# Later pairs of a chunk-attention and MoE kernel: the second product by one-level Strassen too, on weights' factors kept in DRAM

## The chip, the cores and the metric

One core of a Trainium2 chip. The time is the device time of one execution in microseconds (us); the metric is the median of the runs of each kernel. The engines are TensorE (PE), VectorE (DVE), ScalarE (ACT), GpSimd (POOL) and SyncE (SP), which issues all DMAs here.

## What is computed

Attention inside chunks of 64 tokens, then four experts, each weighted by a normalized probability:

```python
# q, k, v: (8, 8, 576, 64); N = 4608 tokens, D = 512, E = 4, F = 1024
scores = 1 / sqrt(64) * q_c @ k_c.T          # in each chunk of 64 tokens
attn = exp(scores - max); attn /= sum(attn) + 1e-9
x = (attn @ v_c) laid out as (4608, 512)
p = domain_probs / (domain_probs.sum(-1) + 1e-9)
for e in range(4):
    h = maximum(x @ w1[e], 0)
    out += p[:, e:e+1] * (h @ w2[e])
```

## The kernel before

The 4608 tokens are one sub-block of 512 and four **pairs** of two sub-blocks (pairs 0 to 3, 1024 tokens each). Half an expert (512 of its 1024 hidden columns) is one **pass**: eight passes for the first sub-block (`plain_pass`), then eight for each pair (`pair_pass`).

Every operand of a matmul is split into a high part, which ACT casts (`hi_part`, L210), and a low part, the difference, on POOL or DVE (`lo_part`, L213). A product of two operands is three matmuls for each block of 128 in the contraction: high x high, high x low, low x high (`TERMS`). A matmul streams 512 columns against a 128x128 block. `product` (L330) issues them all, so they have one line.

For a pair, x w1 is done by one-level Strassen in Winograd's form. The weights are cut into quadrants a11 to a22 with sums s1 to s4 (`Factors`, made by POOL in every pass), the tokens into b11 to b22 with differences t1 to t4 (`Tokens`). Seven products replace eight, each for two groups of 128 hidden columns (`Group(0)` is `g`, `Group(1)` is `h`): g.p1 to g.p7 and h.p1 to h.p7, six matmuls each, 84 in place of 96. The products accumulate in one bank (`self.a`) whose running sums ACT copies out on the way (`keep`, tiles s1, s2, s3; L386), and DVE adds them to other banks (`sum_parts`, L390). ACT and DVE then take ReLU and split the result (`relu_parts`, L339 and L340). The second product h w2 is plain: eight output tiles of 12 matmuls, whose result DVE multiplies by p and adds to `acc` (L462). So a pass of a pair has 84 + 96 = 180 matmuls. The weights of w1 and w2 are loaded and split anew in each pass.

The order is written out by hand. Each engine runs its instructions in the order in which they are issued. A pass is a list of PE steps, numbered from 0, and a table `at` that says behind which step the other work is issued; `issue` walks both. The last step of a pass (`held`) is issued as step 2 of the next one. `Beside` feeds in the attention of the next pair at a fixed rate, one piece at a time: scores, softmax, weights, transpose, values. All loads and stores go through SP's queue, in the order of issue. The PSUM banks come from one pool of six that rotates (`bank`).

## Time and profile before

| | |
|---|---|
| runs: median (lowest to highest) | 1590.95 us (1589.54 to 1591.47) |
| the profiled execution's own time | 1589.11 us |
| its span | 1587.3 us |
| matmuls of a pair's pass | 180 |
| DMA traffic | 123.13 MB, mean 78 GB/s |

The span runs from the first to the last instruction of the profiled execution; its own time has 1.8 us more around it. Rows of a timeline begin with the start in us and the duration; a row of a group has the operands (out <- in), the count, the busy time, the mean of one in ns, the idle time ahead of them and what ended it. The views that carry the argument are quoted in the prediction.

### The profile page before, as it was taken

How to read it: one execution, taken by the hardware profiler on the slowest of the kernel's cores; microseconds unless marked ns; L12 is line 12 of the kernel's file. 1: busy time of each engine (PE TensorE's matmuls, PEld its weight loads, DVE VectorE, ACT ScalarE, POOL GpSimd, SP SyncE). 2: the span in 40 equal slices, each digit the busy share in tenths (PEclk: the TensorE clock that was granted, in tenths of full speed). 3: DMA queues.
4: the chain of work that ended last, by engine and by line, in shares of the span. 5: the costliest groups of instructions: out<-in, count | busy, mean ns of one | idle time of the engine just before them, and what ended most of it. 6: DMA issues, size and time to landing. Idle time of an engine off the chain costs nothing.

```text
span 1587.3 us, 22072 instructions
## 1 busy us (share of the span) xinstructions
PE 1573.1 (99%) x9055; PEld 1285.5 (81%) x9056; DVE 733.1 (46%) x1038; ACT 583.2 (37%) x1037; POOL 737.1 (46%) x554
## 2 busy tenths in 40 slices
PE   7999999999999999999999999999999999999999
PEld 6877878888887888888888888888888888888887
DVE  5444554444444554444444644444444633333333
ACT  3343443333344443333333533333333433333332
POOL 2344574444444463444444744443344744444441
PEclk9999999999999999999999999999999999999999
DMA  5343341122221142221121232212211311111111
GB/s 195 120 140 120 102 151 57 63 74 74 74 74 46 34 147 74 86 75 51 56 73 54 81 139 74 73 50 72 73 54 53 100 48 51 45 51 53 53 40 53
DMA packets 43317, 123.13 MB, mean 78 GB/s; under 512 B 4304, under 2 KB 4688, under 8 KB 43216
## 3 DMA queue, kind: packets, MB, share of 16 engines
q1 hardware_dynamic: 43216, 121.73, 23.1%
q8 instruction: 71, 1.16, 0.3%
q14 instruction: 30, 0.25, 0.0%
...
## 4 chain that ended last, share of the span: by engine, by line
PE 92%; DVE 4%; ACT 2%; issue 1%; POOL 1%; DMA 1%; SPq 0%; POOLq 0%
PE ps L332 88%; PE psa L139 1%; PE psa L105 1%; PE psa L130 1%; DVE hl L340 1%; DVE e L171 1%; ACT hh L339 1%; DVE ps L390 1%; ACT s L386 0%; DMA xraw<-in_qk 0%; POOL w1l L213 0%; DVE z L169 0%; DVE z L164 0%; DMA wraw<-in_w 0%; ACT w1h L210 0%
## 5 line engine op out<-in xcount | busy, mean ns | idle before, releaser
L213 POOL TENSOR_TENSOR w2l<-wraw,w2h 128x512 fp32r<-128x512 f32 x160 | 211.9, 1341 | 629.1 <-ACT w2h L210 628.9
L332 PE MATMUL ps<-w2h,hh 128*128 128x512 f32 x1156 | 452.9, 392 | 0.0
L332 PE MATMUL ps<-w2h,hl 128*128 128x512 f32 x1156 | 449.3, 389 | 0.0
L332 PE MATMUL ps<-w2l,hh 128*128 128x512 f32 x1156 | 449.1, 389 | 0.0
L332 PE MATMUL ps<-xh,w1h 128*128 128x512 f32 (+1 forms) x1040 | 407.9, 393 | 0.6 <-ACT s L386 0.6
L332 PE MATMUL ps<-xh,w1l 128*128 128x512 f32 (+1 forms) x1040 | 401.9, 387 | 0.0
L332 PE MATMUL ps<-xl,w1h 128*128 128x512 f32 (+1 forms) x1040 | 400.1, 387 | 0.6 <-DVE xl L213 0.6
L462 DVE SCALAR_TENSOR_TENSOR acc<-ps,pr,acc 128x512 f32<-128x512 f32 (+1 forms) x253 | 187.4, 746 | 304.0 <-PE ps L332 303.8
L340 DVE SCALAR_TENSOR_TENSOR hl<-ps,hh 128x512 fp32r<-128x512 f32 (+1 forms) x292 | 199.2, 682 | 214.4 <-ACT hh L339 214.2
L213 POOL TENSOR_TENSOR w1l<-wraw,w1h 128x512 fp32r<-128x512 f32 x190 | 255.3, 1366 | 89.8 <-ACT w1h L210 88.0
L386 ACT COPY s<-ps 128x512 f32<-128x512 f32 x192 | 112.9, 588 | 443.1 <-PE ps L332 443.1
L339 ACT ACTIVATE hh<-ps 128x512 fp32r<-128x512 f32 (+1 forms) x292 | 173.2, 593 | 247.8 <-DVE ps L390 171.7
L332 PEld LDWEIGHTS ps<-w2h,hl 128*128 128x128 f32 x1156 | 217.0, 188 | 45.3
L332 PEld LDWEIGHTS ps<-w2h,hh 128*128 128x128 f32 x1156 | 217.0, 188 | 45.2
L332 PEld LDWEIGHTS ps<-w2l,hh 128*128 128x128 f32 x1156 | 217.1, 188 | 43.8
L390 DVE TENSOR_TENSOR ps<-ps,s 128x512 f32<-128x512 f32 x192 | 133.6, 697 | 256.0 <-ACT s L386 180.1
L332 PEld LDWEIGHTS ps<-xh,w1h 128*128 128x128 f32 x1040 | 195.7, 188 | 41.1 <-ACT s L386 1.1
L332 PEld LDWEIGHTS ps<-xh,w1l 128*128 128x128 f32 x1040 | 195.8, 188 | 40.0
L332 PEld LDWEIGHTS ps<-xl,w1h 128*128 128x128 f32 x1040 | 195.0, 189 | 38.7 <-DVE xl L213 1.0
L210 ACT CAST w1h<-wraw 128x512 fp32r<-128x512 f32 x192 | 112.0, 618 | 9.2 <-POOL wraw L242 8.7
L213 POOL TENSOR_TENSOR w1l<-ws,w1h 128x512 fp32r<-128x512 f32 x64 | 84.7, 1343 | 62.8 <-ACT w1h L210 62.7
L210 ACT CAST w2h<-wraw 128x512 fp32r<-128x512 f32 x160 | 95.1, 622 | 1.1 <-DMA wraw<-in_w 1.1
...
## 6 DMA issues: line engine op xcount, KB each, us to landing
wraw<-in_w SPq DMA_DIRECT2D x160, 512.0 KB, 4.0
qk_in<-in_qk SPq DMA_DIRECT2D x32, 512.0 KB, 5.2
out<-acc SPq DMA_DIRECT2D x35, 256.0 KB, 3.8
v_in<-in_v SPq DMA_DIRECT2D x32, 256.0 KB, 4.9
xraw<-in_qk SPq DMA_DIRECT2D x3, 512.0 KB, 10.2
qk_in<-in_v SPq DMA_DIRECT2D x2, 512.0 KB, 9.5
xraw<-in_qk SPq DMA_DIRECT2D x2, 256.0 KB, 2.7
...
```

The costliest lines, as they stand in the source:

```text
L105: nc.tensor.matmul(s["sc"][half, c, j], lhsT=s["x"][rows, g, 0, h], rhs=s["x"][rows, g, 1, h], start=True, stop=True,)
L130: nc.tensor.transpose(ps[:, j], s["e"][:, j].rearrange("p c k -> p (c k)"), ident)
L139: nc.tensor.matmul(av[half, c, j], lhsT=s["v"][rows, 2 * j + odd], rhs=s["pt"][rows, j, half], start=True, stop=True,)
L171: nc.vector.tensor_tensor(out=e, in0=e, in1=z.unsqueeze(2).broadcast_to([P, n, C]), op=ALU.mult)
L210: nc.scalar.copy(out=t[0], in_=src)
L213: eng.tensor_tensor(out=t[1], in0=src, in1=t[0].bitcast(F32), op=ALU.subtract)
L332: nc.tensor.matmul(out, lhsT=lhs(k, a), rhs=rhs(k, b), start=first and i == 0, stop=last and i == len(parts) - 1, skip_group_check=not (fi ...
L339: nc.scalar.activation(out=hi, in_=src, func=AF.Relu)
L340: nc.vector.scalar_tensor_tensor(out=lo, in0=src, scalar=0.0, in1=hi.bitcast(F32), op0=ALU.max, op1=ALU.subtract)
L386: nc.scalar.copy(out=t, in_=self.a)
L390: nc.vector.tensor_tensor(out=out, in0=p, in1=kept, op=ALU.add)
L462: nc.vector.scalar_tensor_tensor(out=o, in0=self.ps, scalar=p_e, in1=o, op0=ALU.mult, op1=ALU.add)
```

## The change

The first sub-block stays as it was but for the shape of its loads and the order in which pair 0's tokens are split. For pairs 1 to 3 the second product is done by Strassen as well, transposed: the output's columns stand on the partitions and the tokens are streamed. That has four parts.

- **Factors once.** In pair 0 (`first_pair_pass`) both w1's and w2's seven factors are made in each pass, split and stored in DRAM (`Factors.keep`): 14 slots of 512 KB for a pass, in the order in which they will be used (`ORDER`). The second product of pair 0 itself stays plain.
- **Streaming.** From pair 1 on nothing of the weights is made. `ring_load` fetches the slots through seven buffers `wf0` to `wf6`; when both halves of a slot have been used (`Units.done`), the load of the slot seven further on is issued.
- **p on h.** The outputs are summed over experts in `acc`, so p is multiplied into h: `Scaled.hidden` takes ReLU times p, where p lies as a row, broadcast over the partitions (`transpose_probs`, `probs_load`). DVE makes the differences t1, t3 and t2 (`sums`), POOL t4 (`last_sum`), ACT all high parts, POOL all low parts. `Outer` does the seven products (`a` for the first, `b` for the second 128 columns of a group) and DVE adds each running sum to `acc` (`Outer.add`). In a pair's first pass ACT copies it.
- **Outputs transposed last.** `outputs` transposes each tile of `acc` on PE, copies and stores it: in the first pass of the next pair, and for the last pair at the end (`last_outputs`).

The six banks now have names and fixed users. `a` and `g` use A0, B0 and C0, `b` and `h` A1, B1 and C1, but for p2's and p7's sums (B0 and B1). `qk_in` and `v_in` have one buffer each instead of two. A pass of pairs 1 to 3 has 168 matmuls, in the 34 steps of `later_pass` below; a step `x.p1(0)` is the first half of a product, three matmuls, and `x.p1(1)` the second.

```diff
-    ps = ctx.enter_context(tc.tile_pool(name="ps", bufs=6, space=bass.MemoryType.PSUM))
+    ps = ctx.enter_context(tc.tile_pool(name="ps", bufs=1, space=bass.MemoryType.PSUM))
-    def bank():
-        return ps.tile([P, SUB], F32, name="ps")
+    BANKS = ("A0", "A1", "B0", "B1", "C0", "C1")
+    turn = [0]
+    def bank(name=None):
+        if name is None:
+            name = BANKS[turn[0] % len(BANKS)]
+            turn[0] += 1
+        return ps.tile([P, SUB], F32, name=name)
...
+    def transpose_probs():
+        by_e = att.tile([P, n_exp, n_tiles], F32, name="e")
+        nc.vector.tensor_copy(out=by_e, in_=pr.rearrange("p t e -> p e t"))
+        by_e = by_e.rearrange("p e t -> p (e t)")
+        psa = ps_a.tile([P, 2, 2 * HG * C], F32, name="psa")
+        rows = att.tile([P, 2, P], F32, name="pt")
+        for i in range(2):
+            n = min(P, p_rows - i * P)
+            nc.tensor.transpose(psa[:n, i, :P], by_e[:, i * P : i * P + n], ident)
+            nc.scalar.copy(out=rows[:n, i], in_=psa[:n, i, :P])
+            nc.sync.dma_start(out=p_t[i * P : i * P + n, :], in_=rows[:n, i])
...
-                if step is a_scores and t + 1 < last:
-                    a_load(t + 1)
                 step(t)
+                if step is a_scores:
+                    a_load_v(t)
+                    if t + 1 < last:
+                        a_load(t + 1)
...
+    KEYS = {"a11": 0, "a12": 1, "a22": 2, "s1": 3, "s2": 4, "s3": 5, "s4": 6}
+    ORDER = [
+        (0, "a11", 0), (0, "a12", 0), (0, "s2", 0), (0, "s1", 0), (0, "a11", 1), (0, "s3", 0),
+        (0, "a12", 1), (0, "s2", 1), (0, "a22", 0), (0, "s4", 0), (0, "s1", 1), (0, "s3", 1),
+        (1, "a11", 0), (1, "a12", 0), (0, "a22", 1), (0, "s4", 1), (1, "a11", 1), (1, "s1", 0),
+        (1, "s1", 1), (1, "a12", 1), (1, "s2", 0), (1, "s2", 1), (1, "s4", 0), (1, "s3", 0),
+        (1, "s4", 1), (1, "s3", 1), (1, "a22", 0), (1, "a22", 1),
+    ]
+    PLACE = {unit: divmod(i, 2) for i, unit in enumerate(ORDER)}
+    N_RING = 7
+    RING = (0, 1, 4, 3, 5, 2, 6)
+    UNIT = [P, 2, 2, P]
+    slots = {
+        (n, i): dram.tile([P, 2, *UNIT[1:]], F32, name=f"w{n}_{i}")
+        for n in range(n_pass) for i in range(N_SLOT)
+    }
...
-        t = raw[i, piece] = wpool.tile([P, 2, HF], F32, name="wraw", bufs=3)
+        t = raw[i, f, k] = wpool.tile([P, 2, 2 * P], F32, name="wraw", bufs=N_RAW)
...
+        def hi(self, name):
+            k = KEYS[name]
+            tag = f"wf{k}"
+            pool = wpool
+            if self.i == 1:
+                tag, pool = f"hf{'hl'[k % 2]}6", hpool
+            t = self.made[name] = pool.tile([P, 2, *UNIT[1:]], F32R, name=tag)
+            parts = [t[:, :, part] for part in range(2)]
+            if self.i == 0:
+                w1t[k] = parts
+            hi_part(by_group(getattr(self, name)), parts)
+        def keep(self, n, name):
+            for g in range(2):
+                to = slot(n, self.i, name, g)
+                if name in self.made:
+                    nc.sync.dma_start(out=to, in_=self.made[name][:, g].bitcast(F32))
+                    continue
+                quad = w2_quad(int(name[1]) - 1, int(name[2]) - 1)
+                for part in range(2):
+                    nc.sync.dma_start(out=to[:, part], in_=quad[part][:, :, g * P : (g + 1) * P].bitcast(F32))
...
+    def ring_load(r):
+        if r < n_ring:
+            ring[r] = wpool.tile([P, 2, *UNIT[1:]], F32R, name=f"wf{RING[r % N_RING]}")
+            nc.sync.dma_start(out=ring[r].bitcast(F32), in_=slots[r // N_SLOT % n_pass, r % N_SLOT])
...
         def p1(self):
-            self.a = bank()
-            self.part(self.a, 0, 0, True)
+            self.a = bank(f"A{self.g}")
+            self.part(self.a, "a11", 0, True)
             self.s1 = self.keep("s1")
...
+    class Units:
+        def __init__(self, n):
+            self.first = (n - 2 * n_pass) * N_SLOT
+            self.left_over = {}
+        def done(self, i, name, g):
+            k, u = PLACE[i, name, g]
+            n = self.left_over[k] = self.left_over.get(k, 2) - 1
+            if n == 0:
+                ring_load(self.first + k + N_RING)
...
+        def hidden(self, src, s, f):
+            i, k = divmod(f, 2)
+            t = self.values[f"b{i + 1}{s + 1}", k] = wpool.tile([P, SUB], F32, name="wraw", bufs=N_RAW)
+            nc.vector.scalar_tensor_tensor(
+                out=t, in0=src, scalar=0.0, in1=self.pb[:, s], op0=ALU.max, op1=ALU.mult
+            )
+        def sums(self, k):
+            self.less("t1", "b12", "b11", k, nc.vector)
+            self.less("t3", "b22", "b12", k, nc.vector)
+            self.less("t2", "b22", "t1", k, nc.vector)
+        def last_sum(self, k):
+            self.less("t4", "b21", "t2", k, nc.gpsimd)
+        def hi(self, name, k):
+            nc.scalar.copy(out=self.part(name, 0)[:, k], in_=self.value(name, k))
+        def lo(self, name, k, eng=None):
+            (eng or nc.gpsimd).tensor_tensor(
+                out=self.part(name, 1)[:, k], in0=self.value(name, k),
+                in1=self.part(name, 0)[:, k].bitcast(F32), op=ALU.subtract,
+            )
...
+        def sum_parts(self, out, p, kept, s, f):
+            nc.vector.tensor_tensor(out=out, in0=p, in1=kept, op=ALU.add)
+            self.hidden(out, s, f)
...
+        def part(self, out, name, right, first, last, ks=(0, 1)):
+            left = self.left(1, name, self.g)
+            product(
+                out, [part for part in PARTS if part[0] in ks],
+                lambda k, a: left[a][:, k], lambda k, b: self.h.part(right, b)[:, k],
+                first=first and 0 in ks, last=last and 1 in ks,
+            )
+            if 1 in ks:
+                self.left.done(1, name, self.g)
+        def add(self, src, i, s):
+            key = self.n // n_pass, 2 * i + self.g + NK * s
+            if key not in acc:
+                acc[key] = opool.tile([P, SUB], F32, name=f"acc{key[1]}")
+                nc.scalar.copy(out=acc[key], in_=src)
+            else:
+                nc.vector.tensor_tensor(out=acc[key], in0=src, in1=acc[key], op=ALU.add)
...
+        def p6(self, *ks):
+            self.part(self.a, "s2", "t2", False, False, ks)
+            if 1 in ks:
+                self.add(self.a, 0, 1)
+        def p4(self):
+            self.part(self.a, "a22", "t4", False, True)
+            self.add(self.a, 1, 0)
...
+    def outputs(pair, i, out_ps, stage, eng=None):
+        s, j = divmod(i, NT)
+        o = out_ps.rearrange("p (m d) -> p m d", d=P)
+        for m in range(NK):
+            nc.tensor.transpose(o[:, m], acc[1 + pair, m + NK * s][:, j * P : (j + 1) * P], ident)
+        if eng is None:
+            nc.scalar.copy(out=stage, in_=out_ps)
+        else:
+            nc.vector.tensor_copy(out=stage, in_=out_ps)
+        t = (1 + pair * PAIR) * NT + i
+        nc.sync.dma_start(out=out[t * P : (t + 1) * P, :], in_=stage)
...
+        for i, name in enumerate(KEYS):
+            add(at, 1 + i, lambda name=name: made.keep(n, name))
+        w2 = Factors(1)
+        add(at, 0, w2.sum1, w2.sum2)
+        add(at, 3, lambda: w2_split(0, 0), lambda: w2_split(0, 1))
+        add(at, 4, lambda: w2_split(1, 0), w2.sum3)
+        add(at, 5, lambda: w2_split(1, 1), w2.sum4)
+        for i, name in enumerate(("s1", "s2", "s3", "s4")):
+            add(at, 6 + i, lambda name=name: w2.hi(name), lambda name=name: w2.lo(name))
+            add(at, 8 + i, lambda name=name: w2.keep(n, name))
+        for i, name in enumerate(("a11", "a12", "a22")):
+            add(at, 13 + i, lambda name=name: w2.keep(n, name))
+            add(at, 3, lambda: w_load(0, n + 1, 0, 0), lambda: w_load(0, n + 1, 0, 1))
+            add(at, 7, lambda: w_load(0, n + 1, 1, 0))
+            add(at, 10, lambda: w_load(0, n + 1, 1, 1))
...
+    def probs_load(pair, e):
+        t = pb[pair, e] = wpool.tile([P, PAIR, SUB], F32, name="ws")
+        r = e * n_tiles + (1 + pair * PAIR) * NT
+        nc.sync.dma_start(
+            out=t.rearrange("p s t -> p (s t)"),
+            in_=p_t[r : r + PAIR * NT, :].rearrange("t p -> (t p)").partition_broadcast(P),
+        )
+    ASIDE = (1, 4, 7, 24, 26, 29, 32)
...
+        steps = [
+            g.p1, g.p2, held, g.p6, g.p5, h.p1, g.p7, h.p2, h.p6, g.p4, g.p3, h.p5, h.p7,
+            lambda: a.p1(0), lambda: a.p2(0), h.p4, h.p3,
+            lambda: a.p1(1), lambda: b.p1(0, 1), lambda: a.p5(0), lambda: b.p5(0),
+            lambda: a.p2(1), lambda: b.p2(0, 1), lambda: a.p6(0), lambda: b.p6(0),
+            lambda: a.p5(1), lambda: b.p5(1), lambda: a.p6(1), lambda: b.p6(1),
+            a.p3, a.p7, b.p3, b.p7, a.p4,
+        ]
...
+        hi(3, "b11", 0)
+        lo(3, "b11", 0)
+        hi(8, "b22", 0)
+        hi(8, "b11", 1)
...
+        add(at, 11, lambda: sc.sums(0))
+        hi(11, "t1", 0)
+        hi(11, "t2", 0)
+        lo(11, "t1", 0)
+        lo(11, "t2", 0)
+        hi(13, "b22", 1)
+        lo(13, "b22", 1)
+        hi(15, "b21", 1)
+        lo(15, "b21", 1)
+        add(at, 16, lambda: sc.sums(1))
...
+        for k in range(2):
+            hi(18, "t3", k)
+            lo(18, "t3", k)
+        for k in range(2):
+            add(at, (12, 22)[k], lambda k=k: sc.last_sum(k))
+            hi((14, 22)[k], "t4", k)
+            lo((14, 22)[k], "t4", k)
...
+        if first_pass and pair > 1:
+            def output(i):
+                stage = att.tile([P, SUB], F32, name=("e", "pt")[i % 2])
+                psa = ps_a.tile([P, 2, 2 * HG * C], F32, name="psa")
+                outputs(pair - 1, i, psa[:, 0], stage)
+            for i in range(PAIR * NT):
+                add(at, (4, 7, 10, 13, 16, 19, 22, 24)[i], lambda i=i: output(i))
...
+        for i, step in enumerate(steps):
+            if step is not None:
+                step()
+            for f in at.get(i, ()):
+                f()
+            if i in ASIDE and not first_pass:
+                beside.go()
+        return b.p4, late
+    def last_outputs():
+        pair = n_pairs - 1
+        ws = wpool.tile([P, 2, SUB], F32, name="ws")
+        stages = [hpool.tile([P, SUB], F32, name=name, bufs=1 + (name == "s2")) for name in ("s1", "s2", "s2", "s3")]
+        stages += [ws[:, 0], ws[:, 1]]
+        stages += [att.tile([P, SUB], F32, name=name) for name in ("e", "pt")]
+        for j, i in enumerate((4, 5, 6, 7, 0, 1, 2, 3)):
+            eng = nc.vector if i < NT and i % 2 else None
+            outputs(pair, i, bank(("B0", "B1", "C0", "C1")[j % NT]), stages[j], eng)
```

In the rows below a matmul names out <- moving operand, stationary operand; numbers behind a name tell tiles apart, and what stands in brackets are the semaphores it waits for: those of DVE, ACT (Activation), POOL, PE or of a DMA (DMAHW).

PE where one pass ends and the next begins, before: the end of a tile (the moving operand is w2), then g.p1 on its own bank.

```order
L332 MATMUL ps_13080<-w2h3_12867,hh13_12953 128x512
L332 MATMUL ps_13080<-w2l3_12868,hh13_12953 128x512
L332 MATMUL ps_13080<-w2h3_12867,hl13_12954 128x512
L332 MATMUL ps_13094<-xh0_10981,w1h0_12916 128x512 [waits DVE_49]
L332 MATMUL ps_13094<-xl0_10982,w1h0_12916 128x512
```

The same place now, between two passes of the last pair: the end of a.p4 and the start of g.p1.

```order
L427 MATMUL A0_13676<-hfh3_13686,wf6_13747 128x512 [waits Activation_49]
L427 MATMUL A0_13676<-hfl3_13688,wf6_13747 128x512 [waits Pool_49]
L427 MATMUL A0_13676<-hfh3_13686,wf6_13747 128x512
L427 MATMUL A0_13828<-xh0_11418,wf0_13706 128x512 [waits DMAHW3_49,DVE_49]
L427 MATMUL A0_13828<-xl0_11419,wf0_13706 128x512
```

The two tiles A0_13676 and A0_13828 are the same bank; DVE's add of the former stands between them.

ACT around h.p7 (the copy to `s3`), before: the ReLU of g.p3's result and casts of the next pass's weights are ahead of it.

```order
L339 ACTIVATE hh02_13215<-ps_13094 128x512 [waits PE_49]
L210 CAST w1h0_13228<-wraw_13103 128x512 [waits DMAHW0_49]
L339 ACTIVATE hh10_13238<-ps_13143 128x512 [waits DVE_49]
L210 CAST w1h1_13244<-wraw_13167 128x512 [waits DMAHW1_49]
L386 COPY s3_13254<-ps_13154 128x512 [waits PE_49,Activation_49]
```

Now, in a pass of the last pair (hfh4 and hfh5 are the high parts of t1 and t2 of h, hfh1 of b21):

```order
L596 CAST hfh1_13936<-wraw_13934 128x512 [waits DVE_49]
L596 CAST hfh4_13961<-wraw_13847 128x512 [waits DVE_49]
L596 CAST hfh5_13963<-wraw_13900 128x512 [waits DVE_49]
L488 COPY s3_13978<-A1_13879 128x512 [waits PE_49,Activation_49]
L596 CAST hfh2_13922<-wraw_13981 128x512 [waits DVE_49]
```

All three casts ahead of the copy now wait for DVE.

ACT in a pass of pair 0, steps 6 to 9, now (before, no such rows stood there): hfl6 and hfh6 hold the factors of w2 in turn, s1 and s3 in hfl6, s2 and s4 in hfh6; hfh1 is the ReLU of g.p4.

```order
L271 CAST hfl6_3692<-ws_3585 128x2x256 [waits DMAHW6_49,Pool_49]
L161 COPY pt_3700<-psa_3695 128x512 [waits PE_49]
L434 ACTIVATE hfh3_3710<-B1_3686 128x512 [waits DVE_49]
L271 CAST hfh6_3716<-ws_3585 128x2x256 [waits DMAHW2_49,Pool_49]
L488 COPY s2_3727<-A1_3666 128x512 [waits PE_49]
L434 ACTIVATE hfh0_3621<-B0_3702 128x512 [waits DVE_49]
L271 CAST hfl6_3733<-wraw_3526 128x2x256 [waits DMAHW7_49,DMAHW6_49,Pool_49]
L434 ACTIVATE hfh1_3742<-A0_3586 128x512 [waits PE_49]
```

The second cast into hfl6 waits for the DMAs that store the first one's result, and the ReLU stands behind it.

## The prediction

> **What bounds the kernel now.** The page comes first: the engines' shares of the span, and the chain that ended last.

> ```profile
> span 1587.3 us, 22072 instructions
> PE 1573.1 (99%) x9055; PEld 1285.5 (81%) x9056; DVE 733.1 (46%) x1038; ACT 583.2 (37%) x1037; POOL 737.1 (46%) x554
> PE 92%; DVE 4%; ACT 2%; issue 1%; POOL 1%; DMA 1%; SPq 0%; POOLq 0%
> ```

> PE is busy throughout and is 92% of the chain; each other engine is idle more than half the time. So the time is the number of matmuls times their pace, and a change moves it by taking matmuls away or by making PE wait. The timeline of PE in a late pass gives the pace: 95 matmuls lie between these two starts (the rows between are evenly spaced).

> ```profile
> 1319.78 0.39 PE L332 MATMUL ps<-w2l,hh 128*128 128x512 f32 x1
> ...
> 1341.31 0.39 PE L332 MATMUL ps<-xh,w1h 128*128 128x512 f32 x1
> ```

> (1341.31 - 1319.78) / 95 = 0.2266 us per matmul; 0.39 is a duration, and durations overlap. A pass of 180 matmuls takes 40.8 us, and one of 168 would take 38.1.

> **Removed: matmuls.** In pairs 1 to 3 (24 passes) the second product takes 14 x 6 = 84 matmuls where it took 96. 24 x 12 x 0.2266 = **-65.3 us**. Splitting the weights in these passes goes too, but POOL and ACT did it beside PE, so that is worth nothing by itself.

> **Added: transposes.** 24 output tiles of four transposes each, all PE work. The chain in order of time shows four such in the attention, and the hand-over from DVE to PE just ahead:

> ```profile
> 590.39 1.51 DVE e L171
> 592.04 0.63 PE psa L130 x4
> 592.67 6.85 PE ps L332 x30
> ```

> 24 x 0.63, and 0.3 for the probabilities: **+15.4 us**. DVE ends at 591.90 and PE starts at 592.04: 0.14 us from DVE to PE.

> **Added: a wait at each pass boundary.** Step 33 (`a.p4`) ends in bank A0 and the next pass's step 0 (`g.p1`) begins in A0, so PE waits for DVE's add of that bank into `acc`. Before, the banks rotated and the last one was long free. The timeline gives the hand-overs:

> ```profile
> 1338.85 0.70 DVE L390 TENSOR_TENSOR ps<-ps,s 128x512 f32<-128x512 f32 x1 [2.02 <-PE ps L332]
> 1339.58 0.60 ACT L339 ACTIVATE hh<-ps 128x512 fp32r<-128x512 f32 x1 [1.56 <-DVE ps L390]
> 1341.09 0.39 PE L332 MATMUL ps<-w2h,hl 128*128 128x512 f32 x1
> 1341.51 0.75 DVE L462 SCALAR_TENSOR_TENSOR acc<-ps,pr,acc 128x512 f32<-128x512 f32 x1 [1.97 <-PE ps L332]
> ```

> DVE starts 0.42 after the start of the last matmul; add 0.70, hand back 0.14: 1.26 instead of 0.23, a wait of 1.03. 23 boundaries: **+23.7 us** (bounds 21 and 28, the latter where DVE is late).

> **Added: `h.p4` (step 15) waits for ACT.** It accumulates in A1, which ACT must first copy to `s3` after `h.p7` (step 12). In ACT's order two casts of step 11 now stand ahead of that copy, and the second waits for the last of five DVE operations behind `g.p3` (step 10): the add, ReLU times p, and the sums t1, t3, t2.

> ```profile
> L386 ACT COPY s<-ps 128x512 f32<-128x512 f32 x192 | 112.9, 588 | 443.1 <-PE ps L332 443.1
> L210 ACT CAST w1h<-wraw 128x512 fp32r<-128x512 f32 x192 | 112.0, 618 | 9.2 <-POOL wraw L242 8.7
> ...
> L340 DVE SCALAR_TENSOR_TENSOR hl<-ps,hh x292: 416/692/694, 23.2 to 1565.9; 128x512 fp32r<-128x512 f32 x142, 128x256 fp32r<-128x256 f32 x4
> ...
> L171 DVE TENSOR_TENSOR e<-e,z x34: 691/693/1506, 11.9 to 1195.5; 128x512 f32<-128x512 f32 x34
> L213 DVE TENSOR_TENSOR xl<-xraw,xh x13: 1225/1712/2371, 198.3 to 1244.6; 128x1024 fp32r<-128x1024 f32 x13
> L213 POOL TENSOR_TENSOR w1l<-wraw,w1h x190: 1267/1296/2282, 12.0 to 1528.4; 128x512 fp32r<-128x512 f32 x190
> ```

> The last four are of the views of single lines, with min/median/max in ns. From the start of `g.p3`'s last matmul: 0.42 + 0.70 + 0.69 + 3 x 0.69, then the cast 0.62, the copy 0.59 and about 0.15 of hand-overs make 5.24. Without the wait `h.p4` starts 19 matmuls later, at 4.31. So PE waits at least 0.93 us. The sums read two SBUF operands while POOL runs, and there the DVE rows spread: 1225 to 2371 ns, 1.15 more at most, median 0.5 more. Three sums at the worst row give 0.93 + 3 x 1.15 = 4.4, but POOL stands still between two of them (it waits for the cast of t1), so two, 3.2, is my upper bound. I take 1.6, one sum between median and worst: 24 x 1.6 = **+38.4 us** (22 to 77).

> [...]

> **Added: `a.p2(1)` (step 21) waits for POOL.** Per pass POOL now makes 14 low parts and two differences. Back to back they take 1.27 each:

> ```profile
> 1344.05 2.54 POOL L213 TENSOR_TENSOR w2l<-wraw,w2h 128x512 fp32r<-128x512 f32 x2 [18.35 <-ACT w2h L210]
> ```

> That is 20.3 us of 38.1, so POOL is no bound, but its order is. From t1's cast (65 x 0.2266 to the start of `g.p3`'s last matmul, then 0.42 + 0.70 + 0.69 + 0.69 and a cast of 0.62: about 18.0 us into the pass) stand six operations up to b21's second low part: 18.0 + 6 x 1.27 = 25.6, and two or three sums push it back by 0.5 to 1.1 each, to 26.6 to 28.9. PE reaches that low part after 112 matmuls, 25.4, and the 1.6 of step 15: 27.0. I take 0.4, near the low end: **+9.6 us** (0 to 46).

> **Moved: attention between the steps.** DVE's share of a tile, from the timeline:

> ```profile
> 236.69 0.68 DVE L115 TENSOR_REDUCE m<-psa 128x8 f32<-128x512 f32 x1
> 237.41 0.69 DVE L116 TENSOR_TENSOR e<-psa,m 128x512 f32<-128x512 f32 x1
> ...
> 244.21 0.68 DVE L164 TENSOR_REDUCE z<-e 128x8 f32<-128x512 f32 x1
> ...
> 245.75 1.49 DVE L171 TENSOR_TENSOR e<-e,z 128x512 f32<-128x512 f32 x1
> ```

> Softmax takes 1.4, the weights 3.0 (244.21 to 247.24). Six passes of pairs 1 and 2 carry them after steps 1, 4, 7, 24, 26, 29, 32. Behind step 7 stand b21 and the chain of t2, behind 26 the add that frees A0, behind 32 the add at the boundary. By the rate of the issue a pair meets these places some six times, at about 1 us each beyond what the waits above already cover: I take **+10 us** (0 to 20) for both pairs, and **+4** (0 to 10) for the two passes in which the next pair's tokens are split on the same engines.

> **Added in the first pair: ACT waits for a DMA.** Its passes keep 180 matmuls, but make and store both weights' factors. w2's s1 and s3 share one buffer, so ACT's cast of s3 (step 8) waits until s1 lies in DRAM, and behind that cast stands the ReLU of `g.p4`, which `begin(0)` (step 13) needs. POOL's first low part stands 1344.05 - 1335.87 = 8.2 us into the pass of before:

> ```profile
> 1335.87 0.39 PE L332 MATMUL ps<-xh,w1h 128*128 128x512 f32 x1
> ...
> out<-acc SPq DMA_DIRECT2D x35, 256.0 KB, 3.8
> wraw<-in_w SPq DMA_DIRECT2D x160, 512.0 KB, 4.0
> ```

> Seven POOL operations (8.9), a store (3.8, as `out`), a cast and a ReLU (1.2) end at 22.1. PE wants that ReLU after 87 matmuls, at 19.7. The wait is 2.4; eight passes, **+19.2 us** (0 if POOL starts early, 32 if the store takes 1.6 more, behind w1's stores).

> **The end** loses its half-width tile and gains copies and 256 KB stores behind the last transposes: **+2 us** (0 to 5).

> **Hidden: the stream.** Each later pass loads 14 x 512 KB, 191 GB/s in 38.1 us. A load is issued when its buffer's last user has run, six slots of twelve matmuls ahead (16 us; 11 for the slot that is freed latest), and takes 4.0. On SP they stand in one order with the attention's loads; the longest holder is the next pair's first `qk_in` load (step 30 of a last pass), which waits some 8 us for POOL's low part of t1 in the next pass, less than the lead. Transfers overlap, in the view of busy time by stretch:

> ```profile
> 22.00:23.00 1.00, 1.00 (x10) 1.00 (x10) 0.00 (x0) 1.00 (x3) 0.00 (x0) 1.00 1.04 397
> ```

> The last number is 397 GB/s, the one before it the DMA engines' share. Cost 0; without overlap, 14 x 4.0 = 56 us a pass (a rival below).

> **Sum** against this execution's own 1589.1 us: -65.3 + 15.4 + 23.7 + 38.4 + 9.6 + 10 + 4 + 19.2 + 2 = +57.0, so 1646.1. The median of the runs shown, 1590.95, is 1.8 higher: **1648 us**. All terms low give 1584, all high 1759.

> **Rivals.**
> *The waits stay at their floor (faster).* If the sums never meet POOL, the wait at step 15 is 0.93, the boundary 0.9, all others 0: -65.3 + 15.4 + 20.7 + 22.3 = -6.9, **1584**. It decides by PE's wait per later pass: with the first pair hidden too, the change wins below 49.9 / 24 = 2.1 us. For it: POOL works only 20.3 us of a pass. Against it: boundary and step 15 alone come to 1.96 at their cheapest.
> *POOL and DVE hold each other up.* Steps 15 and 21 near their upper ends, 3.0 and 1.2: 24 x 2.2 more than taken, **1701**. For it: the 2371 ns row.
> *The clock falls in the waits.* At the start of before, after gaps of PE, the granted clock (last number but two) fell; first the timeline of PE, then the stretches after the gap:

> ```profile
> 26.67 0.63 PE L512 MATMUL ps<-ident,e 128*128 128x128 f32 x4 [2.15 <-DVE e L171]
> ```

> ```profile
> 27.00:28.00 1.00, 1.00 (x8) 1.00 (x7) 0.96 (x2) 0.00 (x0) 0.00 (x0) 0.66 0.92 311
> 28.00:29.00 1.00, 1.00 (x7) 1.00 (x6) 0.18 (x1) 0.79 (x2) 0.00 (x0) 0.50 0.35 139
> 29.00:30.00 1.00, 0.73 (x4) 0.43 (x3) 0.34 (x1) 1.00 (x4) 0.57 (x1) 0.50 0.00 0
> 30.00:31.00 1.00, 0.84 (x20) 0.84 (x22) 0.97 (x3) 0.91 (x3) 1.00 (x2) 0.63 0.00 0
> ```

> A gap of 2.15 us with little beside it cost at most 0.34 + 0.50 + 0.50 + 0.37 = 1.7 us of clock. Once in each of 32 passes: +54, **1702**. Against it: the waits here are mostly 1 to 1.6 us, with 13 us of matmuls between them. [...]
> *The stream binds.* 56 us a pass instead of 41.1: 24 x 14.9 more, **2006**. The 397 GB/s speak against it.

> **Chances.** Forecast (1605 to 1685) 0.66; floor 0.12, of which 0.05 within 0.2%; POOL and DVE 0.12; clock 0.07; stream 0.03. A difference of 0.2%, 3.2 us, is about what a measurement of this kernel can tell from none. Faster 0.08, same 0.05, slower 0.87. The range leaves out the floor, the stream and a few of the highest: **1592 to 1708**.

> **What would show it.** In the profile after: among the waits PE <- DVE `acc` about 23 times 1.0; PE <- ACT `s3` 24 times 1 to 2; PE <- POOL low part under 1; in the first pair PE <- ACT ReLU, eight times 2.4; the clock at 9 throughout; DMA near 200 GB/s with no PE wait on it. The forecast is wrong if PE's idle time in a later pass without attention is below 2 us or above 5.

## The result, and the profile after

| | before | after |
|---|---|---|
| median of the runs (lowest to highest) | 1590.24 us (1586.45 to 1591.47) | 1796.05 us (1793.55 to 1798.35) |
| the profiled execution: span | 1587.3 us | 1792.9 us |

The ratio is 1.1298, with a 95% interval of 1.1272 to 1.1325: the change makes the kernel 13% slower. The prediction had the sign, but 1648 us, and its range ended at 1708.

The page of after, the same lines as of before (spans, busy time and share of each engine, the granted clock of PE in 40 slices, the shares of the chain):

```profile
span 1792.9 us, 23418 instructions
...
PE 1607.1 (90%) x8853; PEld 1272.2 (71%) x8854; DVE 964.6 (54%) x1301; ACT 572.3 (32%) x997; POOL 857.3 (48%) x645
...
PEclk9999989999999999998999899998999899999999
...
PE 15%; DVE 3%; issue 0%; ACT 0%; DVEq 0%
```

Of the page before, the row of the clock:

```profile
PEclk9999999999999999999999999999999999999999
```

There are 202 PE instructions less, yet PE is busy 34 us longer and idle 186 us instead of 14. The idle time shows waits, and a busy time that grows while the work shrinks shows a lower clock: the 8s in its row (over the whole span 0.96 of full speed, 1.00 before). The chain is followed back over only 18% of the span here, so it says little, and the waits have to be read instead. Who PE waited for (total, times, longest):

```profile
PE A L427 <- ACT s L488: 54.0, 24, 3.5
PE A L427 <- DVE acc L645: 27.9, 29, 2.0
PE A L427 <- DVE hfl L435: 22.5, 8, 7.5
PE psa L159 <- DVE e L200: 11.3, 6, 2.6
PE psa L740 <- ACT e L742: 7.3, 2, 3.6
PE A L427 <- DVE acc L720: 6.9, 7, 2.9
...
PE B L427 <- POOL hfl L599: 6.1, 4, 2.6
...
PE psa L98 <- DVE e L92: 4.7, 1, 4.7
```

Three of them are the prediction's own: step 15 (ACT `s`), the boundary (DVE `acc`, L645) and the first pair's ReLU (`hfl`). The others are the attention (`psa` L159), the transposed outputs (L740), boundaries up to and in the first pair (L720) and the transposes of the probabilities (L98).

By stage: busy time of each engine (number of instructions behind it), the granted clock, the DMA engines' share and GB/s, of the first sub-block, pair 0, and pairs 1 to 3, each from the first matmul of its first pass:

```profile
0.00:229.90 229.90, 214.07 (x1644) 171.95 (x1646) 114.36 (x162) 84.18 (x151) 98.61 (x76) 0.98 0.39 123
229.90:622.20 392.30, 360.90 (x1995) 287.61 (x1994) 163.62 (x234) 146.15 (x259) 228.40 (x178) 0.97 0.67 225
622.20:1021.50 399.30, 347.25 (x1884) 270.64 (x1883) 241.71 (x319) 116.47 (x199) 182.95 (x132) 0.95 0.51 168
1021.50:1427.80 406.30, 354.87 (x1921) 277.20 (x1922) 240.78 (x319) 121.16 (x207) 181.84 (x133) 0.94 0.52 170
1427.80:1792.90 365.10, 330.00 (x1414) 264.79 (x1414) 204.07 (x267) 104.38 (x182) 165.52 (x129) 0.97 0.52 169
```

The first number behind the stretch is its length, the next PE's busy time; the difference is idle. The same stages before:

```profile
0.00:223.40 223.40, 214.79 (x1657) 172.90 (x1659) 113.83 (x161) 83.58 (x149) 98.52 (x76) 0.98 0.37 126
223.40:565.00 341.60, 340.52 (x1969) 277.56 (x1968) 163.81 (x232) 131.76 (x234) 169.00 (x126) 1.00 0.23 74
565.00:909.60 344.60, 344.14 (x1985) 280.90 (x1984) 164.68 (x233) 130.17 (x231) 165.21 (x123) 1.00 0.23 74
909.60:1254.30 344.70, 344.26 (x1986) 280.97 (x1985) 164.59 (x233) 130.18 (x231) 165.14 (x123) 1.00 0.23 74
1254.30:1587.30 333.00, 329.40 (x1465) 273.16 (x1463) 126.23 (x179) 107.54 (x193) 139.20 (x110) 1.00 0.16 55
```

Against the prediction's terms, put into their stages:

| stage | predicted | measured | PE idle after |
|---|---|---|---|
| first sub-block | +0.3 | +6.5 | 15.8 |
| pair 0 | +19.2 | +50.7 | 31.4 |
| pair 1 | +9.1 | +54.7 | 52.1 |
| pair 2 | +14.2 | +61.6 | 51.4 |
| pair 3 and the end | +14.2 | +32.1 | 35.1 |
| sum | +57.0 | +205.6 | 185.8 |

**One pass without attention**, a quiet pass below (the fourth of pair 3), tells most of it. It took 43.90 us, where 41.1 was predicted (38.1 and the waits 1.03, 1.6 and 0.4) and 40.8 stood before. The same columns as above for this pass, and below it for the second pass of the pair, which has no stretch at half clock:

```profile
1564.94:1608.84 43.90, 40.58 (x168) 32.44 (x168) 25.57 (x34) 11.71 (x20) 20.30 (x16) 0.96 0.57 181
1477.87:1521.00 43.13, 39.13 (x168) 31.21 (x168) 25.80 (x33) 12.10 (x21) 21.24 (x16) 1.00 0.55 185
```

First its waits; the timeline around step 15 (start, duration, and in brackets the idle time ahead and what ended it):

```profile
1578.72 3.80 POOL L599 TENSOR_TENSOR hfl<-wraw,hfh 128x512 fp32r<-128x512 f32 x3 [5.52 <-ACT hfh L596]
...
1581.86 3.76 DVE L583 TENSOR_TENSOR wraw<-wraw 128x512 f32<-128x512 f32 x3
1583.10 0.62 ACT L596 CAST hfh<-wraw 128x512 fp32r<-128x512 f32 x1 [2.79 <-DVE wraw L583]
1583.80 1.27 POOL L599 TENSOR_TENSOR hfl<-wraw,hfh 128x512 fp32r<-128x512 f32 x1 [1.28 <-ACT hfh L596]
1585.65 0.62 ACT L596 CAST hfh<-wraw 128x512 fp32r<-128x512 f32 x1 [1.93 <-DVE wraw L583]
1586.18 0.58 ACT L488 COPY s<-A 128x512 f32<-128x512 f32 x1
1586.81 0.50 PE L427 MATMUL A<-xh,wf 128*128 128x512 f32 x1 [2.52 <-ACT s L488]
```

The queue is the one foreseen: two casts, then the copy to `s3`, then PE. The size is not. Three sums of 0.69 took 3.76: alone, their rows show 1.21, 0.69 and 1.72. POOL's three low parts run until 1582.52, and the first sum, begun at 1581.86, ends 0.55 after them: it was held for 0.52. The third begins at 1583.89, just behind POOL's low part of t1 (1583.80 to 1585.07), and again ends 0.55 after POOL, at 1585.62: held for 1.03. So the wait is 0.93 + 0.52 + 1.03 = 2.5; PE shows 2.52, and its first matmul takes 0.1 longer to be followed.

Then the clock. In this profile the 34 stretches at half clock (0.50) are one, two or three times 3.413 us long, but for the last of them, and all start on one grid of that step. Two passes of the last pair, cut along that grid (last number but two: the granted clock):

```profile
1583.85:1587.26 3.41, 0.90 (x4) 0.43 (x4) 2.20 (x2) 1.10 (x2) 2.13 (x2) 1.00 0.54 159
1587.26:1590.67 3.41, 3.41 (x10) 2.63 (x9) 1.61 (x3) 1.70 (x3) 3.32 (x4) 0.50 0.00 0
1495.10:1498.51 3.41, 2.11 (x10) 1.41 (x8) 3.27 (x3) 0.62 (x1) 1.60 (x2) 1.00 0.61 195
1498.51:1501.92 3.41, 2.21 (x10) 1.83 (x11) 1.85 (x4) 1.82 (x4) 2.61 (x3) 1.00 0.05 20
1501.92:1505.34 3.42, 3.42 (x17) 2.84 (x16) 2.65 (x5) 1.37 (x3) 3.42 (x3) 1.00 0.44 141
```

The same wait of 2.5 us stands in both. In the first two rows it falls into one cell of the grid, PE is busy for 0.90 of it, and the next cell runs at half clock (10 matmuls, where the fifth row, busy throughout at full clock, has 17). In the other three rows it is split over two cells, neither is idle for more than 1.3, and the clock stays at 1.00.

### The profile page after: what moved, and what is told of

Its sections match the earlier page's. It is cut to its first block, busy times and chain, and to the rows that moved or that the text cites. A ratio compares the mean times of both kernels' runs of the same rounds, so it can differ in the third digit from the quotient of the medians.

```text
span 1792.9 us, 23418 instructions
## 1 busy us (share of the span) xinstructions
PE 1607.1 (90%) x8853; PEld 1272.2 (71%) x8854; DVE 964.6 (54%) x1301; ACT 572.3 (32%) x997; POOL 857.3 (48%) x645
## 3 DMA queue, kind: packets, MB, share of 16 engines
q8 instruction: 70, 1.15, 0.3%
## 5 line engine op out<-in xcount | busy, mean ns | idle before, releaser
L599 POOL TENSOR_TENSOR hfl<-wraw,hfh 128x512 fp32r<-128x512 f32 x336 | 444.3, 1342 | 632.6 <-ACT hfh L596 631.2
L427 PE MATMUL A<-xh,wf 128*128 128x512 f32 (+1 forms) x1128 | 399.7, 408 | 82.6 <-ACT s L488 54.0
L427 PEld LDWEIGHTS A<-xh,wf 128*128 128x128 f32 x1128 | 217.6, 194 | 150.3 <-ACT s L488 64.3
L596 ACT CAST hfh<-wraw 128x512 fp32r<-128x512 f32 x336 | 200.6, 620 | 378.8 <-DVE wraw L583 216.6
L427 PE MATMUL A<-hfh,wf 128*128 128x512 f32 x768 | 278.0, 406 | 10.8 <-DVE acc L645 9.1
L427 PE MATMUL A<-xl,wf 128*128 128x512 f32 (+1 forms) x564 | 224.8, 400 | 0.0
L427 PE MATMUL C<-xh,wf 128*128 128x512 f32 (+1 forms) x584 | 204.0, 403 | 0.0
L427 PEld LDWEIGHTS A<-hfh,wf 128*128 128x128 f32 x768 | 147.4, 192 | 53.8 <-DVE acc L645 13.5
L583 DVE TENSOR_TENSOR wraw<-wraw 128x512 f32<-128x512 f32 x144 | 174.2, 1209 | 9.9
L274 POOL TENSOR_TENSOR hfl<-wraw,hfh 128x512 fp32r<-128x512 f32 x64 | 87.4, 1387 | 162.1 <-ACT hfh L271 162.0
L645 DVE TENSOR_TENSOR acc<-A,acc 128x512 f32<-128x512 f32 x174 | 117.2, 686 | 72.5 <-PE A L427 72.5
L427 PE MATMUL A<-hfl,wf 128*128 128x512 f32 x384 | 153.2, 399 | 0.0
L617 DVE TENSOR_TENSOR B<-C,s 128x512 f32<-128x512 f32 x48 | 33.6, 700 | 146.0 <-ACT s L488 146.0
L645 DVE TENSOR_TENSOR acc<-C,acc 128x512 f32<-128x512 f32 x90 | 61.4, 688 | 60.5 <-PE C L427 53.8
## 6 DMA issues: line engine op xcount, KB each, us to landing
wf<-w SPq DMA_DIRECT2D x336, 512.0 KB, 3.9
wraw<-in_w SPq DMA_DIRECT2D x128, 256.0 KB, 3.9
w<-wf SPq DMA_DIRECT2D x112, 256.0 KB, 4.3
qk_in<-in_qk SPq DMA_DIRECT2D x32, 512.0 KB, 4.2
v_in<-in_v SPq DMA_DIRECT2D x32, 256.0 KB, 4.0
w<-hfl SPq DMA_DIRECT2D x32, 256.0 KB, 2.3
w<-hfh SPq DMA_DIRECT2D x32, 256.0 KB, 3.0
```

The source lines that it names most:

```text
L274: eng.tensor_tensor(out=t[1], in0=src, in1=t[0].bitcast(F32), op=ALU.subtract)
L427: nc.tensor.matmul(out, lhsT=lhs(k, a), rhs=rhs(k, b), start=first and i == 0, stop=last and i == len(parts) - 1, skip_group_check=not (fi ...
L583: eng.tensor_tensor(out=self.value(name, k), in0=self.value(a, k), in1=self.value(b, k), op=ALU.subtract)
L596: nc.scalar.copy(out=self.part(name, 0)[:, k], in_=self.value(name, k))
L599: (eng or nc.gpsimd).tensor_tensor(out=self.part(name, 1)[:, k], in0=self.value(name, k), in1=self.part(name, 0)[:, k].bitcast(F32), op=AL ...
L617: nc.vector.tensor_tensor(out=out, in0=p, in1=kept, op=ALU.add)
```

## Experiments

All runs are compared with the kernel before, on the same chip; "lost clock" is half the length of the half-clock stretches (74.8 us after, 4.5 before).

**The copy ahead of the casts.** In the later passes the casts of t1 and t2, and POOL's low parts, are issued behind step 12:

```diff
-        hi(11, "t1", 0)
-        hi(11, "t2", 0)
-        lo(11, "t1", 0)
-        lo(11, "t2", 0)
+        hi(12, "t1", 0)
+        hi(12, "t2", 0)
+        lo(12, "t1", 0)
+        lo(12, "t2", 0)
```

> In the later passes ACT's casts of t1 and t2 (first half) and POOL's low parts of them are issued behind step 12, so that the copy to s3 no longer stands behind them. Theory A (the wait of PE at step 15 is only this queue on ACT): the waits PE <- ACT s3 fall from 54.0 us in 24 to under 8, nothing replaces them, and with the half-clock stretches that follow them the time falls from 1796 by 54 + 4 + some 35 to about 1703 (1685 to 1725). Theory B (POOL's row is the next bound): t1's cast now ends about 19 us into a pass, and the six POOL operations from t1's low part to b21's second low part end 2.6 us behind the place where PE reaches step 21; PE waits there for POOL's low part, 24 times about 2.6, and the time stays at 1785 to 1805. I hold B the likelier.

Measured: 1756.23 us (ratio 1.1042, 1.1015 to 1.1070). The wait for `s` is gone from the list of PE's waits, and this row stands at its head:

```profile
PE B L427 <- POOL hfl L599: 51.1, 25, 2.6
```

The mechanism is theory B's: 51.1 for 54.0, at step 21 instead of 15. Its time, 1785 to 1805, was missed, and theory A's too. The 40 us that were won are not this wait: lost clock fell from 74.8 to 54.2 (the granted clock of the run is 0.970, and 0.959 after), and with PE late at step 21 the wait at step 23 (below) is covered. How the 40 divide among these wasn't measured. The prediction's step 15 was therefore never one wait to be taken away: behind it POOL's row was as late.

**POOL and DVE apart.** Two POOL operations change places:

```diff
-        lo(11, "t1", 0)
         lo(11, "t2", 0)
+        lo(11, "t1", 0)
```

> Only the order of two POOL operations is changed: the low part of t2 stands ahead of that of t1, so POOL waits for t2's cast and stands still while DVE makes the third sum. If DVE's sums are long because POOL holds them (three take 3.76 us in a quiet pass, against 2.07 alone), the three take about 2.6, PE's wait at step 15 falls from 2.5 to about 1.4 us, and some 0.7 of that comes back at step 21 as a wait for POOL. If they are long for another reason (slower reads, ACT's traffic), the three stay at 3.7 and the wait at 2.5. On the clock: if what counts is the idle time of PE within one stretch of 3.41 us of a fixed grid (over about 1.9), no pass without attention has such a stretch any more and their half-clock stretches go; with both, 1796 falls by about 10 for the waits and 25 to 35 for the clock, to 1750 to 1765. If the clock falls after any gap over 1 us, the stretches stay and the time is about 1785.

Measured: 1787.18 us (ratio 1.1238, 1.1212 to 1.1265). The three sums in a pass without attention, and PE's waits:

```profile
1620.64 2.73 DVE L583 TENSOR_TENSOR wraw<-wraw 128x512 f32<-128x512 f32 x3
```

```profile
PE A L427 <- DVE acc L645: 39.0, 42, 3.2
PE A L427 <- ACT s L488: 33.0, 24, 2.5
...
PE B L427 <- POOL hfl L599: 21.7, 21, 2.6
```

3.76 became 2.73 by nothing but POOL standing still during the third sum (its row ends at 1621.30 and goes on at 1624.10), and the wait in such a pass 1.47 instead of 2.52. So the sums were long because POOL worked beside them: now it works beside the first alone. With the shorter wait the granted clock of the run is 0.975 instead of 0.959, and lost clock falls to 46 us. But the time moved by only 9 us, where 31 to 46 were expected: 0.91 of 1.05 came back at step 21, and the DVE wait at step 23, 0.7 us, which half clock had covered before, now shows in every pass (42 waits for `acc` instead of 29). A quiet pass took 43.2 instead of 43.9.

**The wait filled.** In the last pair nine more matmuls, whose result nobody reads, stand ahead of step 15:

```diff
+        def fill(self):
+            left, right = self.left(1, "a11", self.g), self.h.part("b11", 0)
+            psa = ps_a.tile([P, SUB], F32, name="psa")
+            for _ in range(9):
+                nc.tensor.matmul(psa, lhsT=left[0][:, 0], rhs=right[:, 0], start=True, stop=True)
...
+        if pair == n_pairs - 1:
+            add(at, 14, a.fill)
```

> In the eight passes of the last pair nine more matmuls (2.0 us, into a bank that nobody reads) are put ahead of step 15, where PE waits 2.5 us; nothing else is changed. Theory: the half clock follows from PE's idle time in the stretch before, and costs 1.7 us each time. Then of the last pair's half-clock stretches (6 of 24 to 29 us together now, 10.7 us lost) all but those at the end of the program go, a quiet pass takes 42.2 to 43.1 us where it took 43.9, and the time falls by 6 to 10 us to about 1788, though PE does 72 matmuls more. Rival: the half clock has another cause (power, DMA traffic, or the waits are shorter than what trips it): the stretches stay, and the time stays at 1796 or rises by up to 4.

Measured: 1797.62 us (ratio 1.1290, 1.1266 to 1.1315), no gain. The clock did what the theory said: this quiet pass, from start to start, has a granted clock of 1.00, where the one above had 0.96. Below it PE's waits over the six quiet passes:

```profile
1571.08:1614.30 43.22, 41.20 (x178) 32.91 (x178) 26.42 (x34) 11.62 (x20) 21.28 (x16) 1.00 0.56 183
```

```profile
PE A L427 <- DVE acc L651: 9.2, 12, 0.8
PE A L427 <- ACT s L488: 2.9, 6, 0.5
```

But 43.90 became 43.22, not 42.2: a stretch of 1.71 us lost is worth only 0.7. Part of the rest is the wait at step 23, about 0.7, which a slower PE doesn't have: the waits for `acc` in these passes are now 12, and were 8. The change itself shows the same without any filling: its two quiet passes without half clock take 43.1, the other four 43.7 to 43.9. In the pair's first pass the fill cost more than it won: there it and the transposed outputs share a bank, and the pass took 5.3 us longer. So the clock is real and follows the waits, but of the 70 us more that are lost only a part is time.

**Other banks at the end.** The last two steps of a later pass change places, and one tile of the first pair uses another bank:

```diff
-            a.p3, a.p7, b.p3, b.p7, a.p4,
+            a.p3, a.p7, b.p3, a.p4, b.p7,
-    TILE_BANKS = ("A0", "C0", "B0", "A1", "C1", "B1", "A0", "C1")
+    TILE_BANKS = ("A0", "C0", "B0", "A1", "C1", "B1", "C0", "C1")
```

> The last two steps of a later pass change places (a.p4 ahead of b.p7), and tile 6 of the first pair's passes uses bank C0 instead of A0, so that neither bank A0 is the last one used before g.p1. Theory: the boundary wait is the hand-over PE to DVE to PE on one bank, 0.95 us (0.78 idle and 0.17 of an unpipelined matmul) in the later pairs and 1.0 in the first; 23 and 7 of them go, none comes back, as six matmuls (1.36 us) now cover the 1.26 of the add: about 29 us less, 1767. Rival: DVE is late at this place (attention, sums), so the wait only moves to a.p4 behind a.p7, where one group of six stands between instead of two: half comes back, 1780.

Measured: 1763.31 us (ratio 1.1078, 1.1055 to 1.1100), 33 less than after: the theory, and a little more. PE's waits for DVE's `acc` in this run:

```profile
PE A L427 <- DVE acc L645: 10.9, 12, 2.0
...
PE A L427 <- DVE acc L720: 2.9, 1, 2.9
```

They were 27.9 and 6.9, and lost clock didn't fall (76.2; granted clock 0.957). The boundary's 23.7 was sized rightly; the same wait at the seven boundaries of the first pair, 0.2 to 0.84 each and 4.8 in all, was overlooked. The 2.9 that is left stands ahead of the first pair, behind the first sub-block.

**The first pair: the ReLU, and the store.** First only the order on ACT:

```diff
-            add(at, 6 + i, lambda name=name: w2.hi(name), lambda name=name: w2.lo(name))
+            add(at, (6, 7, 9, 10)[i], lambda name=name: w2.hi(name), lambda name=name: w2.lo(name))
```

> First pair only: the casts and low parts of w2's s3 and s4 are issued one step later (behind steps 9 and 10 instead of 8 and 9), so that the ReLU of g.p4 stands ahead of the cast that waits for the store of s1. Theory: the 22.5 us that PE waits there in eight passes (A <- DVE hfl) come from that queue on ACT alone; they go, with eight restarts and most of the first pair's half-clock stretches (13 us lost there), and the time falls by 22 + 2 + 8 to about 1764. Rival: ACT is held up to 9 us there, and what stands behind it now (the copy to s3 of h.p7, which h.p4 needs at step 15) is late in its place; then PE waits for ACT s3 in the first pair, some 1 us a pass, and the time falls by 15 to 20 only, to 1778.

Measured: 1787.08 us (ratio 1.1227, 1.1208 to 1.1245), a gain of 9 where 18 to 32 were expected: a miss. In the first pair PE and ACT waited for:

```profile
PE C L427 <- DVE hfl L435: 22.1, 8, 6.7
```

```profile
ACT hfl L271 <- DMA w<-hfl: 29.5, 8, 6.0
```

In the change ACT waited there 42.1 us, and PE at bank A for 22.5. The wait went from the ReLU of g.p4 to that of g.p3: whichever stands behind the cast is late, since the cast still waits for the store. The next run keeps this order, and splits and stores s1 and s2 ahead of w2's quadrants:

```diff
+        for i, name in enumerate(("s1", "s2", "s3", "s4")):
+            add(at, (3, 3, 9, 10)[i], lambda name=name: w2.hi(name), lambda name=name: w2.lo(name))
+            add(at, (5, 6, 10, 11)[i], lambda name=name: w2.keep(n, name))
         add(at, 3, lambda: w2_split(0, 0), lambda: w2_split(0, 1))
...
-        for i, name in enumerate(("s1", "s2", "s3", "s4")):
-            add(at, 6 + i, lambda name=name: w2.hi(name), lambda name=name: w2.lo(name))
-            add(at, 8 + i, lambda name=name: w2.keep(n, name))
```

> As the run before, and in addition w2's s1 and s2 are split and stored ahead of the four quadrants, so that their buffers are long free when s3 and s4 want them. If the store is what holds ACT (the first theory of the run before), ACT's wait for the DMA (42 us in eight passes) goes and nothing of the wait comes back: 1760 or less, at least as fast as the run before. If it is POOL's row that is late, the quadrants' low parts now come 2.6 us later and PE waits for them at step 13: 1775 to 1785.

Measured: 1765.67 us (ratio 1.1098, 1.1082 to 1.1115), 30 less than after. Of ACT's waits for the stores into both buffers 6.8 us are left, and of PE's:

```profile
PE C L427 <- DVE hfl L435: 7.2, 5, 4.4
```

So the first pair's wait is the shared buffer that a DMA has to empty, as predicted, and an earlier store takes it away where a later ReLU does not.

**The later passes reordered.** The queues of all three engines are put into the order in which PE wants the parts, with the other banks from above:

```diff
-            self.less("t4", "b21", "t2", k, nc.gpsimd)
+            self.less("t4", "b21", "t2", k, nc.vector)
...
+        hi(7, "b22", 0)
+        lo(7, "b22", 0)
...
         add(at, 11, lambda: sc.sums(0))
+        add(at, 11, lambda: sc.last_sum(0))
+        for name in ("t1", "t2"):
+            hi(12, name, 0)
+            lo(12, name, 0)
...
+        add(at, 17, lambda: sc.less("t1", "b12", "b11", 1, nc.vector))
+        add(at, 17, lambda: sc.less("t3", "b22", "b12", 1, nc.vector))
...
+        add(at, 18, lambda: sc.less("t2", "b22", "t1", 1, nc.vector))
...
+        lo(18, "t3", 0)
+        lo(18, "t3", 1)
+        add(at, 22, lambda: sc.last_sum(1))
+        hi(24, "t4", 1)
+        lo(25, "t4", 0)
+        lo(25, "t4", 1)
```

> Later passes only (and bank C0 for tile 6 of the first pair): the last two steps exchanged as in the run with other banks; t1's and t2's casts behind the copy to s3 as in the run with the copy first; and POOL's row in the order in which PE wants the parts (b21's second part ahead of t4, b22 and t3), t4 made by DVE, and DVE's second three sums behind the add that frees A0 for step 23. Theory: four waits make a quiet pass long (2.67 at step 15, 0.95 at the boundary, 0.88 at step 23, and POOL at step 21 once the first is gone); without them it takes 38.1 + 0.5, so 38.4 to 39.0 where it took 43.9; 24 passes by some 4.8, the first pair's 7, and the clock make 1796 - 115 - 7 - 30 = about 1645 (1625 to 1670). Rival: POOL and DVE have no room for it (POOL's 14 low parts and DVE's eight sums hold each other up), and a quiet pass stays above 40.5: 1690 or more.

> The reordered later passes and the early s1 and s2 together. If the waits of the first pair and of the later pairs are independent, the gains add up: about 1645 - 36 = 1609 (1585 to 1635). Against the kernel before (1591) that is still 0 to 2% slower, because the passes with attention keep waits that this version doesn't touch (PE for DVE's weights, for ACT's copies of the attention and of the outputs).

Measured: 1662.96 us (ratio 1.0453, 1.0438 to 1.0469) for the later passes alone and 1631.39 us (1.0249, 1.0231 to 1.0267) with the first pair's edit, each some 20 us above what was expected and within its range. The gains add up: that edit wins 32 here and won 30 alone. A quiet pass of the latter:

```profile
1464.00:1502.25 38.25, 38.25 (x170) 31.46 (x168) 25.40 (x36) 11.54 (x20) 18.80 (x14) 1.00 0.60 193
```

This row carries the study: 43.90 us with 40.58 busy at clock 0.96 became 38.25, all of it busy, while the stream ran at 193 GB/s (five of the six quiet passes are like this; one took 39.5). The second product by Strassen does save its 12 matmuls, and the stream is hidden. Pair 3, without attention, is now faster than before, 323.2 us against 333.0; the pairs that carry attention aren't, and these waits were left there:

```profile
PE psa L159 <- DVE e L200: 16.5, 6, 3.2
PE C L427 <- DVE B L617: 12.1, 7, 2.4
PE C L427 <- DVE hfl L435: 8.4, 5, 5.6
PE C L427 <- DVE acc L645: 8.1, 4, 3.3
```

All four are waits for DVE.

**Attention in DVE's gaps.** A quiet pass leaves DVE idle in two places, some 5 us behind the held step and 2 at the boundary. The attention goes there, with three smaller moves:

```diff
+    LATER_STEPS = (a_scores, a_softmax, a_sum, a_divide, a_transpose, a_values)
...
+    FIRST, BASE = (29, 33), (3, 5, 13, 17, 29, 33)
+    MORE, BEHIND = (3, 5, 7, 8, 13, 14, 25, 27, 31, 32, 33), (2, 4, 5, 13, 17, 29, 33)
+    PIECES = (FIRST, BASE, MORE, BEHIND, MORE, BEHIND, BASE, ())
-            if i in ASIDE and not first_pass:
-                beside.go()
+            if i in PIECES[n % n_pass]:
+                next(beside.steps, None)
...
-        add(at, 11, lambda: sc.last_sum(0))
+        add(at, 12, lambda: sc.last_sum(0))
...
-            add(at, 23, lambda: x.lo("b11"))
-            add(at, 25, lambda: x.lo("t2"))
+            add(at, 8, lambda: x.lo("b11"))
+            add(at, 33, lambda: x.lo("t2"))
...
-            add(at, (3, 3, 9, 10)[i], lambda name=name: w2.hi(name), lambda name=name: w2.lo(name))
+            add(at, (3, 3, 9, 11)[i], lambda name=name: w2.hi(name), lambda name=name: w2.lo(name))
```

> The version before this with four more edits. The next pair's attention in pairs 1 and 2 is cut into six pieces a tile (the weights' sum and division apart) and placed where DVE is idle in a quiet pass (about 5 us behind the held step, 2 us at the boundary) instead of at seven places of which four lie among DVE's adds; t4's difference stands behind the sum that frees C1; in a last pass two of the tokens' operations on DVE go to the boundary and one to the front; in the first pair the cast of s4 stands behind the ReLU of g.p3. Theory: what is left against the kernel before (1631 against 1591) are PE's waits for DVE in the passes with attention (some 24 us a pair in pairs 1 and 2, 7.5 in the first two passes of pair 0) with 17 us of half clock behind them; about two thirds go: 1631 - 30 - 12 = 1589 (1575 to 1605), so about as fast as the kernel before. Rival: DVE is simply full in those passes, and the waits only change their names: 1620 or more.

Measured: 1577.16 us, ratio 0.9927 (0.9912 to 0.9941): 0.7% faster than the kernel before, at the fast end of what was expected. DVE was not full, since it still does the same work. Four edits went together here, so the 54 us are not divided among them, and that the attention's places made most of it is likely but not shown.

**The probabilities later.**

```diff
-        transpose_probs()
         for i in range(2, NT):
             o[i].whole()
+        transpose_probs()
```

> The version before this, and the transposes of the probabilities (in the first sub-block's first pass) stand behind the last two output tiles instead of ahead of them. Theory: the change's 4.7 us wait there (PE psa <- DVE e) is only DVE's copy standing behind two low parts of w1 that wait for their loads; behind 5.4 us of matmuls it is hidden, and one half-clock stretch may go with it: 1577 - 4.7 = 1572 (1569 to 1575). Rival: PE would wait for those low parts anyway at the start of the next pass, and the wait moves there: 1576 to 1578.

Measured: 1573.66 us, ratio 0.9895 (0.9878 to 0.9912), 3.5 of the 4.7 us hoped for; 1.0 of the wait is left. This version is 1% faster than the kernel before. Its page:

```profile
span 1572.1 us, 23451 instructions
...
PE 1532.8 (97%) x8853; PEld 1246.1 (79%) x8854; DVE 955.3 (61%) x1349; ACT 568.7 (36%) x997; POOL 802.9 (51%) x597
...
PEclk9999999999999999999999999999999999999999
```

PE runs the same 8853 matmuls as in the change, in 74 us less of busy time, and idles 39 us instead of 186.

## Why the prediction was wrong, step by step

- **Removed matmuls, -65.3.** Right: a reordered quiet pass is 38.25 us against 40.80, 2.55 of the 2.72.
- **Transposes, +15.4.** About right: in the reordered version the first pass of pairs 2 and 3, with eight output tiles, takes 42.8 us and a quiet one 38.2, so 4.6 for the 5.0 reckoned. In the change PE also waited twice 3.6 for ACT's copies of them (`psa` L740), a wait that the sum left out.
- **The boundary, +23.7.** Right in size. The run with other banks won 33 for 23 boundaries of the later pairs and seven of pair 0, which the prediction had left out.
- **Step 15, +38.4: the step that failed first.** "I take 1.6, one sum between median and worst" drew one value from a spread of rows. Nothing in a quiet pass is spread: the order fixes where POOL stands, and in all six the three sums take 1.21, 0.69 and 1.72, so the first is held for half a POOL operation and the third for most of one. The wait is 2.5 us in each; 54.0 in all, and each restart costs some 0.1 more. The working had named an upper bound (two sums held, 3.2) and taken half of it. The runs show the holding: of the 144 sums of the change the 88 that take over 0.8 us all end 0.54 to 0.55 us after the POOL operation in which they began, and the swap, which takes one hold away, shortens the three sums by 1.03.
- **Step 21, +9.6.** The total is right by luck: 10.7 (6.1, and two waits of 2.3 put down to a DMA at places where other runs name POOL), but in six waits of 0.6 to 2.6 in the passes of pairs 1 and 2 and in no quiet pass, because PE was late. As the run with the copy first shows, it is worth 51 as soon as step 15 is cured.
- **Step 23: missing.** `a.p6` accumulates in A0 behind `a.p1`, whose add DVE makes only after the second three sums. The wait is 0.7 us where the clock is full, and nothing where half clock covers it.
- **The clock, a rival with 0.07 at 1702: it came together with the forecast's waits, not instead of them.** "The waits here are mostly 1 to 1.6 us, with 13 us of matmuls between them" fell with step 15: where the 2.5 us lie in one cell of the grid, the next cell is at half clock (the cell with 0.90 us of work), and with 1.47 (the swapped low parts) the granted clock of the run rose from 0.959 to 0.975. The rival was priced at 1.7 us, which is just the cost of one stretch (3.41 us at 0.50). The net price is smaller than the loss: 0.7 of 1.7 in a quiet pass. In the passes with attention it wasn't separated. The prediction's own sign of being wrong, an idle time of PE below 2 or above 5 us in a quiet pass, missed it: the idle time is 3.3, as forecast, and the clock is in the busy time, 40.6 instead of 38.1. "The clock at 9 throughout" was the sign that failed.
- **Attention, +10, and token passes, +4.** The largest error of a single term. The first six passes with attention in pair 1 take 50.4 us on average against 43.4 before, 3.9 more than the growth of a quiet pass, and each last pass 52.4 against 40.8. Over two pairs that is some 60 us, with the clock that these passes lose in it. The estimate counted six meetings a pair at 1 us. Moving the pieces, with three other edits, gave 54 back from a version whose quiet passes were already cured, so the pieces (up to 3 us of DVE each) probably stood ahead of adds and sums that PE was waiting for; which of them met which wasn't followed.
- **The first pair, +19.2.** The mechanism is right (the cast waits for the store, the ReLU for the cast): 26.5 us with the waits at bank C, instead of 19.2. The surplus is in the first two and the last pass (7.5, 4.2 and 5.2 where 2.4 was taken); why wasn't settled. The seven boundaries (4.8) and 13 us of lost clock make most of the rest of +50.7.
- **The probabilities, +0.3.** 4.7 us: PE waited for DVE's copy, and with the transposes issued later 1.0 of it is left. Most of the rest of the first sub-block's +6.5 is the wait of 2.9 at its end.
- **The stream, 0.** Right: a quiet pass at 193 GB/s has no idle PE.

So the sign was right for the reasons given, and the sum failed in three places: a wait that the order fixes was taken as an average, attention was priced on a queue that was thought to have room, and the clock was treated as an alternative although it follows from the waits. Of the 148.6 us that the sum was short, a quiet pass 2.8 us longer than forecast makes some 67 over 24 passes (step 15, step 23 and the clock), attention some 46, pair 0 31.5 and the first sub-block 6.
